# Gated linear attention from a hand-written list of steps: the front half of the list in another order

## The chip, the core and the metric

The kernel runs on one core of a Trainium2 chip. The metric is the device time of one execution in microseconds; the time before is the median of three runs. The engines are TensorE (PE, with its weight loads, PEld), VectorE (DVE), ScalarE (ACT), GpSimd (POOL) and SyncE (SP), which here only issues DMAs.

## The reference

Eight batches, eight heads, 576 tokens, 64 values a head; the model width is 512.

```python
q_s = np.exp(q - np.max(q, axis=-1, keepdims=True)); q_s = q_s / (np.sum(q_s, axis=-1, keepdims=True) + 1e-09)
k_s = np.exp(k - np.max(k, axis=2, keepdims=True));  k_s = k_s / (np.sum(k_s, axis=2, keepdims=True) + 1e-09)
kv = np.einsum('bhsd,bhse->bhde', k_s, v)
x  = np.einsum('bhsd,bhde->bhse', q_s, kv)          # then (batch, token, 512)
gate_pre = sum(conv_w[j] * x shifted by 4 - j tokens, j = 0 to 4)
gate = 1.0 / (1.0 + np.exp(-gate_pre))
out = (gate * (x @ w_val)) @ w_out
```

## The kernel before

The function lists its whole program in `ORDER`, 968 steps by name with a batch, a block of 128 channels and often a letter for the engine (a is ScalarE, v VectorE, p GpSimd). A loop calls the step's function for each, and no scheduler moves anything: every engine works through its own instructions in the order of the list, and waits, with all that stands behind, for data and for buffers. SyncE issues the loads and stores in the list's order too, and each DMA waits for the one eight places earlier.

One batch runs through these steps. `load_q`, `load_k`, `load_v` and others bring the data. The maximum of k over tokens is taken from strided loads (`load_km`, `k_peak`), goes to DRAM and back (`k_row`, `k_spread`) and is subtracted on GpSimd (`k_sub`), then ScalarE takes the exponential (`k_exp`, and `kt_exp` for the last 64 tokens). The first two batches take k by channels instead (`load_kc`, `k_top` on VectorE, `k_raise` on ScalarE) and turn it on TensorE (`k_turn`, `k_turned`). For q there are the maximum per head (`q_max`, VectorE), `q_sub` (GpSimd), `q_exp` (ScalarE) or `q_each` (both at once, ScalarE), the sums (`q_sum` or `q_total`, VectorE), and for batches 0 to 2 the scaling `q_mul`; `q_turn` transposes q on TensorE and `q_turned` copies it out of PSUM as `qT`. From batch 3 on `qT` comes from loads by channels (`load_qc`, `l_sub`, `c_exp`) with the logarithm of the sums (`q_log`, `l_turn`, `l_row`, `l_spread`).

`kv` is 80 matmuls; `kv_sums` and `kv_norm` on VectorE make `ks` and `kvd`. `attend` makes two blocks of x, 16 matmuls. Each block of x is split into a high part (`x_high`, a cast) and a low part (`x_low`, VectorE). The convolution of a block starts with `first` (one tap as a scaled copy), then three or four `tap`s on VectorE that add into the same tile `gate`; a `far` on ScalarE with a `near` on GpSimd can take a tap's place. For blocks 0 and 1 of batch 0 the convolution is made on TensorE (`conv_rows`, `conv_kv`, `conv`, tiles `dg`, `rows`, `cv`). `sigmoid` is a tanh on ScalarE (`conv_gate` for batch 0's two). `value` is a product of 24 matmuls with w_val, in three kinds (high part with low and high weights, low part with high weights); `gated` multiplies on VectorE (tile `g`), `g_high` and `g_low` split the result (`gh`, `gl`), `project` is the 24 matmuls with w_out, `copy` brings the result out of PSUM and `put` stores it.

The weights and tap weights arrive as 64-bit words. For each of eight slabs `part`, `field`, `scaled`, `signed` (two VectorE instructions) and `joined` build the float, and `w_high` and `w_low` split it; slabs 0 to 3 are w_val, 4 to 7 w_out. In the trace their tiles are `words`, `e` and `f`.

Buffers set further bounds: PSUM has four banks that rotate through all products in the list's order; `g` has two buffers, `gh` and `gl` four, the pair of x six, `gate` and `f` six, the big loads of q, k and v two each.

Of the kernel before, what the change touches and what calls it, by code (L numbers as in the profile page):

```python
# [37 lines left out]
    k_turn 0 1, load_km 2 2, load_words 2, field 1 p, q_each 0 0, conv_rows, signed 0, q_rec 0 2 5, scaled 1 a,
    q_mul 0 4 p, k_turned 0 1 v, k_turn 0 0, q_mul 0 2 p, load_km 2 1, k_tail_turn 0, q_sum 0 0 2, k_turned 0 0 a,
    q_eps 0 0 2 a, signed 1, load_kc 1 0, tail_turn 0, q_rec 0 0 2, part 1 a, load_kc 1 2, joined 1 v,  # L40
    tail_turned 0 v, load_q 1 0 5, k_tail_turned 0 a, kv 0, q_mul 0 1 a, k_peak 2 1, q_mul 0 0 p, q_mul 0 3 p,
    part 2 a, k_top 1 0, field 2 p, tail_high 0 a, k_top 1 2, kv_sums 0, q_turn 0 0, load_words 5, kv_norm 0 v,
# [1 line left out]
    joined 2 p, attend 0 0, field 5 p, w_high 1 a, q_max 1 0 2, attend 0 1, w_low 1 p, x_high 0 0 a, w_high 0 p,
    field 6 p, x_high 0 1 a, x_low 0 0, scaled 5 a, load_kc 1 1, w_low 0 p, load_words 7, first 0 3 a, load_km 2 3,
    joined 3 p, x_low 0 1, part 5 p, x_high 0 3 a, k_raise 1 2, field 7 p, q_max 1 2 4, tap 0 3 0, x_high 0 2 a,
    w_high 2 a, tap 0 3 2, conv, tap 0 3 1, q_each 1 3, first 0 2 a, tap 0 3 3, x_low 0 3, k_peak 2 2, q_sub 1 1 p,
    x_low 0 2, k_top 1 1, q_each 1 2, conv_gate 1, tail_high 1 p, k_peak 2 3, value 0 1, k_raise 1 0, signed 5,
    value 0 0, q_sub 1 0 p, load_kc 1 3, gated 0 1, q_exp 1 0 1, k_top 1 3, q_exp 1 1 2, load_vt 2, k_raise 1 1,
    load_words 4, joined 5 p, field 4 p, conv_gate 0, w_high 3 a, part 4 a, k_raise 1 3, q_sum 1 2 4, q_sum 1 0 2,  # L50
    q_eps 1 0 2 a, gated 0 0, scaled 4 p, q_rec 1 0 2, q_eps 1 2 4 a, signed 4, w_low 2 p, w_low 3 p, joined 4 p,
    k_turn 1 0, k_peak 2 0, tap 0 2 2, tap 0 2 1, load_km 3 0, q_mul 1 0 p, load_q 2 0 5, g_high 0 0 a, g_high 0 1 a,
# [704 lines left out]
```

## Time and profile before

| What | Time |
|---|---|
| median of three runs | 290.89 us (290.66 to 292.46) |
| the profiled execution | 291.31 us |
| its span in the profile | 289.5 us |
| busy: TensorE | 268.6 us (93% of the span) |
| busy: VectorE | 234.4 us (81%) |
| busy: GpSimd | 206.0 us (71%) |
| busy: ScalarE | 190.2 us (66%) |

The span begins with the first instruction of the profile and ends with the last; all times in rows are from the span's start. Time at which an engine is idle matters only where the engine that sets the end waits for it. The stretches that the rows use are these: 13.5 us is the first matmul, 34.9 us about the first value product, 143.4 us the kv products of batch 4, 286.5 us the last matmul.

### The profile page before, as it was taken

Reading aid. Unit: us, or ns where it says so; the run is one execution under the profiler, and the core shown is the slowest. Engines: PE = TensorE matmul, PEld = TensorE weight load, DVE = VectorE, ACT = ScalarE, POOL = GpSimd, SP = SyncE. Lnnn points to the kernel's source line nnn. Section 1 sums busy time; section 2 is a strip of 40 time slices with the busy share of each in tenths; the row PEclk is TensorE's granted clock in tenths of the full one; section 3 lists DMA queues with packets and bytes.
Section 4 is the critical chain, followed back from the end, with each engine's and each line's share of the span. In section 5 each row is a group of like instructions: output and inputs, shape, how many; then the busy total and the mean of one; then the engine's idle time right before and its main releaser. Section 6 shows DMA issues by size and latency. Waiting matters only on the chain.

```text
span 289.5 us, 6594 instructions
## 1 busy us (share of the span) xinstructions
PE 268.6 (93%) x2616; PEld 249.0 (86%) x2616; DVE 234.4 (81%) x334; ACT 190.2 (66%) x314; POOL 206.0 (71%) x187
## 2 busy tenths in 40 slices
PE   0188999899999999999999999999999999999995
PEld 0156599789998899898998898999989899989995
DVE  1999999999989979979788989799758974759620
ACT  2798989877598778563886774687936642655002
POOL 3657988789998989799299994879479284443300
PEclk9999999999999999999999999999999999999999
DMA  7999668988679799988869959954554800112022
GB/s 226 404 409 395 202 224 325 283 284 286 178 255 332 215 288 315 351 265 198 246 210 368 247 170 317 367 176 115 159 180 114 223 34 2 43 41 82 2 80 83
DMA packets 23462, 62.92 MB, mean 217 GB/s; under 512 B 3432, under 2 KB 3976, under 8 KB 20744
## 3 DMA queue, kind: packets, MB, share of 16 engines
q1 hardware_dynamic: 23432, 62.51, 66.0%
q8 instruction: 20, 0.33, 0.5%
q14 instruction: 10, 0.08, 0.1%
HBM read 52.96 MB, written 9.54 MB: 216 GB/s over the span
## 4 chain that ended last, share of the span: by engine, by line
PE 61%; DVE 18%; POOL 7%; ACT 5%; DMA 4%; issue 3%; SPq 0%; POOLq 0%; DVEq 0%; ACTq 0%
PE out_a L593 26%; PE val L593 26%; DVE gate L568 5%; PE kv L484 4%; PE x L543 4%; DMA out<-o 2%; DVE qs L412 2%; POOL k L318 2%; DVE e L263 2%; DVE kpk L303 1%; DMA words<-in_w_val 1%; DVE e L262 1%; DMA qc<-in_q_channels 1%; DVE ktop L339 1%; DVE g L652 1%
## 5 line engine op out<-in xcount | busy, mean ns | idle before, releaser
L593 PE MATMUL val<-x,w_val_hi 128*128 128x288 f32 x512 | 88.8, 295 | 0.0
L568 DVE SCALAR_TENSOR_TENSOR gate<-x,cw,gate 128x573 f32<-128x573 f32 (+3 forms) x98 | 78.4, 810 | 7.7 <-ACT gate L556 2.7
L593 PEld LDWEIGHTS val<-x,w_val_hi 128*128 128x128 f32 x512 | 75.2, 188 | 0.0
L593 PE MATMUL val<-x,w_val_lo 128*128 128x288 f32 x256 | 56.4, 301 | 0.6 <-DVE x L563 0.5
L593 PE MATMUL out_a<-gh,w_out_lo 128*128 128x288 f32 x248 | 54.6, 301 | 0.0
L593 PE MATMUL out_a<-gh,w_out_hi 128*128 128x288 f32 x248 | 53.2, 295 | 0.0
L660 POOL TENSOR_TENSOR gl<-g,gh 128x576 fp32r<-128x576 f32 x25 | 35.8, 1435 | 14.8 <-ACT gh L168 7.1
L593 PEld LDWEIGHTS out_a<-gh,w_out_lo 128*128 128x128 f32 x248 | 39.4, 188 | 5.3 <-ACT o L174 1.8
L593 PE MATMUL out_a<-gl,w_out_hi 128*128 128x288 f32 x248 | 43.2, 295 | 0.2 <-POOL gl L660 0.2
L593 PEld LDWEIGHTS val<-x,w_val_lo 128*128 128x128 f32 x256 | 40.7, 188 | 2.7 <-POOL f L176 1.0
L174 ACT ACTIVATE o<-out_a 128x576 f32<-128x576 f32 x27 | 17.6, 651 | 35.2 <-PE out_a L593 22.2
L593 PEld LDWEIGHTS out_a<-gh,w_out_hi 128*128 128x128 f32 x248 | 39.8, 188 | 0.0
L577 POOL TENSOR_TENSOR gate<-gate,far 128x573 f32<-128x573 f32 (+3 forms) x22 | 28.6, 1306 | 15.2 <-ACT far L573 7.6
L383 POOL TENSOR_TENSOR q<-q,qm 128x512 f32<-128x512 f32 x32 | 33.1, 1052 | 5.3 <-DVE qm L378 5.2
L593 PEld LDWEIGHTS out_a<-gl,w_out_hi 128*128 128x128 f32 x248 | 36.4, 188 | 0.4 <-POOL gl L660 0.4
L453 POOL TENSOR_TENSOR qc<-qc,lb 128x576 f32<-128x576 f32 (+1 forms) x17 | 24.7, 1465 | 13.6 <-DMA lb<-lrow 5.6
L652 DVE SCALAR_TENSOR_TENSOR g<-gate,val 128x576 f32<-128x576 f32 x32 | 23.9, 750 | 11.4 <-PE val L593 8.7
L318 POOL TENSOR_TENSOR k<-k,kmax 128x512 f32<-128x512 f32 x23 | 30.0, 1324 | 0.2
L563 DVE TENSOR_TENSOR x<-x,x 128x576 fp32r<-128x576 f32 x32 | 23.2, 750 | 1.8 <-ACT x L168 1.6
L573 ACT ACTIVATE far<-x,cw 128x574 f32<-128x574 f32 (+3 forms) x22 | 16.3, 739 | 12.4 <-PE x L543 4.8
L580 ACT ACTIVATE gate<-gate 128x576 f32<-128x576 f32 x30 | 19.8, 684 | 6.3 <-DVE gate L568 6.1
L556 ACT ACTIVATE gate<-x,cw 128x576 f32<-128x576 f32 x23 | 16.9, 742 | 6.7 <-PE x L543 5.0
(109 smaller groups left out, 443.2 us busy)
## 6 DMA issues: line engine op xcount, KB each, us to landing
out<-o SPq DMA_DIRECT2D x31, 288.0 KB, 2.8
v<-in_v SPq DMA_DIRECT2D x8, 1040.0 KB, 7.5
q<-in_q SPq DMA_DIRECT2D x7, 1024.0 KB, 7.6
km<-in_k_strided SPq DMA_DIRECT2D x24, 288.0 KB, 6.1
k<-in_k SPq DMA_DIRECT2D x6, 1024.0 KB, 6.3
qc<-in_q_channels SPq DMA_DIRECT2D x16, 288.0 KB, 7.7
lb<-lrow SPq DMA_DIRECT2D x8, 576.0 KB, 7.7
kc<-in_k_channels SPq DMA_DIRECT2D x8, 288.0 KB, 5.8
```

The lines of the kernel that those rows point to most:

```text
L174: nc.scalar.mul(out, in_, factor)
L318: engine(e).tensor_sub(kk[r, cs], kk[r, cs], mx[r, cs])
L383: engine(e).tensor_tensor(qq, qq, m, op=ALU.add if b < 2 else ALU.subtract)
L453: engine(e).tensor_sub(t, t, T["lb", b][:, p])
L556: nc.scalar.activation(a, x, AF.Copy, scale=w)
L563: nc.vector.tensor_sub(xl, T["x", b, p], T["xh", b, p].bitcast(F32))
L568: nc.vector.scalar_tensor_tensor(out=a, in0=x, scalar=w, in1=a, op0=ALU.mult, op1=ALU.add)
L577: nc.gpsimd.tensor_add(a, a, T["far", b, p, j])
L580: nc.scalar.activation(T["gate", b, p], T["gate", b, p], AF.Tanh, scale=0.5)
L593: nc.tensor.matmul(ps[:, cs], a[:, kb, ms], z[:, cs], start=(i == 0), stop=(i == len(parts) - 1))
L652: nc.vector.scalar_tensor_tensor(out=T["g", b, m], in0=T["gate", b, m], scalar=1.0, in1=T["val", b, m], op0=ALU.add, op1=ALU.mult)
L660: engine(e).tensor_sub(T["gl", b, m], T["g", b, m], T["gh", b, m].bitcast(F32))
```

## The change

Only `ORDER` differs, its lines 33 to 94, the first 551 steps. The remaining 417, from `k_spread 5, l_sub 4 3 p, kv 4` on, are the same. The functions are the same, and the steps of the front half are the same in number, except where a step changes its engine (54 of them, of the kinds `x_high`, `g_high`, `q_turned`, `k_turned`, `first`, `copy`, `q_mul`, `scaled`, `part`, `w_high`, `tail_high`) or a tap its way (`tap` or `far` with `near`; as many of each as before). Two lines of the 62, of before and after:

```diff
-    load_words 6, load_km 2 0, scaled 2 a, q_turn 0 1, conv_kv, q_turned 0 0 a, joined 0 p, signed 2, q_turned 0 1 a,
+    kv_sums 0, load_kc 1 2, field 2 p, scaled 2 p, kv_norm 0 v, q_turn 0 1, load_q 1 0 5, part 2 a, load_words 4,
```

In the instruction rows that follow, a name has the program's tile with its batch and block where it has them, and a number that tells buffers apart.

ScalarE, from the last two words passes of w_val to the casts of x in batch 0 (`e` and `f` are word slabs, `kc` is k by channels, `x_3` the product and `x_0_3` its split), before:

```order
L174 ACTIVATE f_299<-words_182 128x512
L168 COPY qT_305<-qTt_241 128x4x64
L174 ACTIVATE e_303<-e_303 128x512
L168 COPY qT_305<-qTps_0_311 128x2x512
L168 COPY qT_305<-qTps_1_329 128x2x512
L168 CAST w_val_hi<-f_236 128x4x128
L168 CAST x_0_0_371<-x_0_345 128x576
L168 CAST x_0_1_376<-x_1_346 128x576
L174 ACTIVATE e_355<-e_355 128x512
L556 ACTIVATE gate_3_385<-x_3_361,cw 128x576
L168 CAST x_0_3_393<-x_3_361 128x576
L343 ACTIVATE kc_2_238<-kc_2_238,ktop_301 128x576
```

After the change the same engine has these rows there:

```order
L174 ACTIVATE f_305<-words_144 128x512
L174 ACTIVATE f_328<-words_215 128x512
L168 COPY qT_252<-qTps_0_296 128x2x512
L168 COPY qT_252<-qTps_1_317 128x2x512
L168 CAST x_0_1_353<-x_1_342 128x576
L168 CAST x_0_0_355<-x_0_341 128x576
L556 ACTIVATE gate_3_370<-x_3_358,cw 128x576
L168 CAST x_0_3_377<-x_3_358 128x576
L168 CAST w_val_hi<-f_328 128x4x128
L168 CAST w_val_hi<-f_305 128x4x128
L556 ACTIVATE gate_2_388<-x_2_357,cw 128x576
```

The pass of `e` ahead of the two copies of `qT` is GpSimd's now, the other pass of `e` stands later in the list, and the cast of `w_val_hi` and the second of its kind stand behind the casts of x and the `first` of block 3.

VectorE, the same stage, before:

```order
L262 TENSOR_SCALAR e_303<-e_303 128x512
L263 SCALAR_TENSOR_TENSOR e_303<-words_182,e_303 128x512
L378 TENSOR_REDUCE qm_358<-q_243 128x16
L563 TENSOR_TENSOR x_0_0_371<-x_0_345,x_0_0_371 128x576
L563 TENSOR_TENSOR x_0_1_376<-x_1_346,x_0_1_376 128x576
L378 TENSOR_REDUCE qm_358<-q_243 128x16
L568 SCALAR_TENSOR_TENSOR gate_3_385<-x_3_361,cw,gate_3_385 128x572
L568 SCALAR_TENSOR_TENSOR gate_3_385<-x_3_361,cw,gate_3_385 128x574
L568 SCALAR_TENSOR_TENSOR gate_3_385<-x_3_361,cw,gate_3_385 128x573
L568 SCALAR_TENSOR_TENSOR gate_3_385<-x_3_361,cw,gate_3_385 128x575
L563 TENSOR_TENSOR x_0_3_393<-x_3_361,x_0_3_393 128x576
```

After the change the same engine has these rows there:

```order
L262 TENSOR_SCALAR e_312<-e_312 128x512
L263 SCALAR_TENSOR_TENSOR e_312<-words_215,e_312 128x512
L266 ISA f_305<-e_206,f_305 128x1024
L378 TENSOR_REDUCE qm_367<-q_326 128x16
L563 TENSOR_TENSOR x_0_1_353<-x_1_342,x_0_1_353 128x576
L563 TENSOR_TENSOR x_0_0_355<-x_0_341,x_0_0_355 128x576
L378 TENSOR_REDUCE qm_367<-q_326 128x16
L568 SCALAR_TENSOR_TENSOR gate_3_370<-x_3_358,cw,gate_3_370 128x573
L568 SCALAR_TENSOR_TENSOR gate_3_370<-x_3_358,cw,gate_3_370 128x574
L568 SCALAR_TENSOR_TENSOR gate_3_370<-x_3_358,cw,gate_3_370 128x575
L568 SCALAR_TENSOR_TENSOR gate_3_370<-x_3_358,cw,gate_3_370 128x572
L563 TENSOR_TENSOR x_0_3_377<-x_3_358,x_0_3_377 128x576
```

The join of a slab (`ISA`, tile `f`) stands between the word steps and the maximum of q; four taps of one block follow each other in both.

VectorE, around the sums of batch 1's kv (`ks`, `kvd`), before:

```order
L378 TENSOR_REDUCE qm_650<-q_580 128x40
L303 TENSOR_REDUCE kpk_658<-km_2_655 128x1
L652 SCALAR_TENSOR_TENSOR g_2_697<-gate_2_455,val_2_620 128x576
L170 COPY qT_473<-qTps_0_687 128x2x512
L493 TENSOR_SCALAR ks_755<-kv_711 128x4
L494 RECIPROCAL ks_755<-ks_755 128x4
L500 TENSOR_TENSOR kvd_762<-kv_711,ks_755 128x256
L652 SCALAR_TENSOR_TENSOR g_3_764<-gate_3_385,val_3_661 128x576
```

After the change the same engine has these rows there:

```order
L170 COPY k_577<-kps_1_631 128x4x256
L378 TENSOR_REDUCE qm_684<-q_627 128x40
L652 SCALAR_TENSOR_TENSOR g_2_689<-gate_2_388,val_2_641 128x576
L652 SCALAR_TENSOR_TENSOR g_3_709<-gate_3_370,val_3_597 128x576
L493 TENSOR_SCALAR ks_754<-kv_713 128x4
L494 RECIPROCAL ks_754<-ks_754 128x4
L500 TENSOR_TENSOR kvd_757<-kv_713,ks_754 128x256
L303 TENSOR_REDUCE kpk_771<-km_2_693 128x1
```

The copy of `qT` has left the place ahead of `ks`, and the gate product `g_3` has come ahead of it.

ScalarE, around the exponentials of k of batch 3 (L322) and of q of batch 4 (L387), before:

```order
L174 ACTIVATE o_1_1442<-out_1_a 128x576
L573 ACTIVATE far_2_3_1446<-x_2_1346,cw 128x575
L322 ACTIVATE k_1088<-k_1088 128x2048
L168 COPY qT_1462<-qTt_1205 128x4x64
L580 ACTIVATE gate_0_1255<-gate_0_1255 128x576
L174 ACTIVATE o_2_1499<-out_2_a 128x576
L387 ACTIVATE q_1299<-q_1299 128x2560
L456 ACTIVATE qT_1462<-qc_1_1361 128x512
```

After the change the same engine has these rows there:

```order
L174 ACTIVATE o_1_1490<-out_1_a 128x576
L580 ACTIVATE gate_1_1270<-gate_1_1270 128x576
L168 COPY qT_1501<-qTt_1124 128x4x64
L580 ACTIVATE gate_0_1268<-gate_0_1268 128x576
L387 ACTIVATE q_1334<-q_1334 128x2560
L322 ACTIVATE k_584<-k_584 128x2048
L456 ACTIVATE qT_1501<-qc_0_1389 128x512
L580 ACTIVATE gate_3_1367<-gate_3_1367 128x576
```

The exponential of k has moved from four places ahead of that of q to directly behind it. On TensorE the kv products of batch 3 stand behind three value products of batch 2 after the change, before it behind one.

## Rows read from the trace of the kernel before

**Rows 1.** by stretch: `start:end` in us and length, then busy us by engine, granted clock, DMA

```profile
13.50:34.90 21.40, 18.66 (x240) 13.01 (x240) 20.72 (x32) 20.20 (x50) 16.38 (x18) 1.00 0.90 345
34.90:143.40 108.50, 106.97 (x1016) 100.30 (x1016) 100.27 (x139) 81.58 (x138) 94.26 (x83) 1.00 0.85 270
143.40:286.50 143.10, 142.98 (x1361) 135.69 (x1360) 106.07 (x151) 81.72 (x115) 88.53 (x71) 1.00 0.48 153
```

**Rows 2.** TensorE's waits over the run: total us, times, longest us

```profile
PE kps L350 <- ACT kc L343: 13.5, 1, 13.5
...
PE cv L639 <- DVE x L563: 0.7, 1, 0.7
```

**Rows 3.** TensorE timeline: start us, duration us, line, operation, count, [idle before <-releaser]

```profile
34.94 0.51 PE L593 MATMUL val<-x,w_val_lo 128*128 128x288 f32 x2 [0.49 <-DVE x L563]
...
53.75 1.09 PE L509 MATMUL qTps<-ident,q 128*128 128x128 f32 x8
55.64 1.20 PE L543 MATMUL x<-qT,kvd 64*64 64x288 f32 x16 [0.79 <-DVE kvd L500]
...
108.35 0.69 PE L484 MATMUL kv<-v,k 128*64 128x65 f32 x16 [0.38 <-issue]
...
125.13 0.53 PE L593 MATMUL out_a<-gl,w_out_hi 128*128 128x288 f32 x2 [0.18 <-POOL gl L660]
```

**Rows 4.** ScalarE (ACT) and GpSimd (POOL) timeline around 23 to 30 us

```profile
24.15 0.64 ACT L174 ACTIVATE e<-e 128x512 f32<-128x512 f32 x1 [0.31 <-POOL e L253]
...
26.49 0.63 ACT L168 CAST w_val_hi<-f 128x512 fp32r<-128x512 f32 x1
...
28.94 0.63 ACT L174 ACTIVATE e<-e 128x512 f32<-128x512 f32 x1 [0.65 <-POOL e L253]
29.48 0.73 ACT L556 ACTIVATE gate<-x,cw 128x576 f32<-128x576 f32 x1
...
23.45 0.67 POOL L253 TENSOR_SCALAR e<-words 128x512 f32<-128x512 f32 x1
```

**Rows 5.** VectorE (DVE) timeline: conv stage, around 54 us, around 99 us

```profile
20.88 0.69 DVE L266 CUSTOM_DVE_ANT_0 f<-e,f 128x1024 uint16<-128x1024 uint16 x1
...
25.73 0.42 DVE L262 TENSOR_SCALAR e<-e 128x512 int32<-128x512 int32 x1
...
26.80 1.21 DVE L378 TENSOR_REDUCE qm<-q 128x16 f32<-128x1024 f32 x1
27.92 1.41 DVE L563 TENSOR_TENSOR x<-x,x 128x576 fp32r<-128x576 f32 x2
29.25 1.21 DVE L378 TENSOR_REDUCE qm<-q 128x16 f32<-128x1024 f32 x1
30.77 3.37 DVE L568 SCALAR_TENSOR_TENSOR gate<-x,cw,gate 128x572 f32<-128x572 f32 x4 [0.30 <-ACT x L168]
34.05 0.75 DVE L563 TENSOR_TENSOR x<-x,x 128x576 fp32r<-128x576 f32 x1
...
53.53 1.22 DVE L170 COPY qT<-qTps 128x1024 f32<-128x1024 f32 x1
54.66 0.15 DVE L493 TENSOR_SCALAR ks<-kv 128x4 f32<-128x4 f32 x1
...
99.26 0.81 DVE L568 SCALAR_TENSOR_TENSOR gate<-x,cw,gate 128x574 f32<-128x574 f32 x1
99.99 0.75 DVE L563 TENSOR_TENSOR x<-x,x 128x576 fp32r<-128x576 f32 x1
```

**Rows 6.** ScalarE, VectorE and SyncE queue (SPq) timeline, 86 to 110 us

```profile
103.49 1.91 ACT L322 ACTIVATE k<-k 128x2048 f32<-128x2048 f32 x1
...
109.73 2.34 ACT L387 ACTIVATE q<-q 128x2560 f32<-128x2560 f32 x1 [1.47 <-POOL q L383]
...
96.54 2.81 DVE L378 TENSOR_REDUCE qm<-q 128x40 f32<-128x2560 f32 x1
...
86.90 0.33 SPq L206 DMA_DIRECT2D q<-in_q  x1
```

More of the change, by code (lines that the diff above doesn't have):

```diff
@@ L38 @@
[L38 to L42, printed above, removed]
@@ L43 @@
-    load_words 6, load_km 2 0, scaled 2 a, q_turn 0 1, conv_kv, q_turned 0 0 a, joined 0 p, signed 2, q_turned 0 1 a,
[L44 to L52, printed above, removed]
@@ new lines @@
+    q_each 1 3, conv, w_low 1 p, q_sub 1 1 p, w_high 3 p, w_high 0 a, w_low 3 p, tap 0 3 2, x_high 0 2 a, tap 0 3 3,
+    load_km 2 0, part 5 a, w_low 0 p, load_kc 1 1, tap 0 3 0, load_kt 2, load_words 7, scaled 5 a, x_low 0 3,
+    k_top 1 1, k_top 1 2, conv_gate 1, x_low 0 2, q_exp 1 1 2, k_top 1 0, value 0 1, k_raise 1 1, scaled 4 a,
+    value 0 0, load_km 2 3, tap 0 2 0, signed 5, tap 0 2 2, gated 0 1, k_raise 1 0, field 6 p, load_kc 1 3,
+    q_each 1 2, q_sub 1 0 p, tail_high 1 a, part 4 a, joined 5 p, conv_gate 0, k_top 1 3, k_turn 1 0, q_sum 1 2 4,
@@ new lines @@
+    scaled 7 p, g_low 0 0 p, part 6 a, q_turn 1 0, gated 0 3, q_turned 1 0 a, w_low 5 p, kv 1, kv_sums 1,
+    kv_norm 1 v, g_high 0 2 a, q_turn 1 1, w_low 4 p, k_peak 3 2, g_low 0 2 p, scaled 6 a, attend 1 0, k_peak 4 3,
+    q_turned 1 1 a, g_high 0 3 a, first 1 0 a, g_low 0 3 p, signed 6, load_k 2, first 1 1 a, tap 1 0 3, tap 1 0 1,
+    load_q 3 0 5, tap 1 1 3, joined 6 p, project 0 1, x_high 1 0 a, w_high 6 a, tap 1 0 0, tap 1 1 0, copy 0 1 a a,
+    k_spread 2, x_high 1 1 a, tap 1 0 2, q_sub 2 4 p, project 0 0, x_low 1 0, w_low 6 p, load_km 6 2, tap 1 1 1,
@@ new lines @@
+    put 0 1, attend 1 1, q_sub 2 3 p, copy 0 0 a a, part 7 a, tap 1 1 2, x_high 1 3 a, load_vt 2, signed 7,
+    x_low 1 1, load_vt 4, q_sub 2 2 p, joined 7 p, first 1 2 a, q_sub 2 0 p, x_low 1 3, x_high 1 2 a, q_sub 2 1 p,
+    load_km 4 1, project 0 2, far 1 2 2, x_low 1 2, load_km 4 2, w_high 7 a, load_v 2, w_low 7 p, tap 1 2 1,
+    q_max 3 0 4, value 1 0, k_sub 2 1 p, q_sub 3 1 p, load_km 3 3, tap 1 2 3, k_sub 2 4 p, sigmoid 1 0, first 1 3 a,
+    copy 0 2 a a, project 0 3, q_exp 2 0 5, gated 1 0, q_sum 2 0 5, k_peak 3 0, kt_exp 2, q_sub 3 0 p, q_eps 2 0 5 a,
@@ new lines @@
+    copy 1 0 a a, k_peak 5 0, first 2 3 a, x_high 2 2 a, l_row 3, tap 2 0 1, tap 2 0 2, k_sub 3 3 p, x_low 2 0,
+    q_max 4 0 5, k_sub 3 0 p, first 2 2 a, put 1 3, put 1 0, far 2 0 0, load_v 4, k_sub 3 4 p, load_qc 3 0,
+    project 1 2, k_peak 5 1, project 1 1, q_sub 4 3 p, x_low 2 2, q_sub 4 2 p, x_high 2 3 a, tap 2 2 1, l_spread 3,
+    tap 2 3 1, x_low 2 3, copy 1 2 a a, value 2 1, tap 2 2 2, q_sub 4 1 p, near 2 0 0, tap 2 3 3, k_peak 5 3,
+    kt_exp 3, q_sub 4 0 p, k_peak 6 1, q_sub 4 4 p, copy 1 1 a a, sigmoid 2 1, gated 2 1, tap 2 3 0, g_high 2 1 p,
```

88 lines of the change are left out of this document (41 added, 47 removed).

## The prediction

> **What bounds the kernel now.** I read the busy time of each engine by stretch first [rows 1]. Up to 13.5 us TensorE has nothing to do (it waits for ScalarE's last raised block of k, [rows 2]). From 13.5 to 34.9 us it works 18.66 of 21.4 us, from 34.9 to 143.4 us 106.97 of 108.5 us, and from 143.4 to 286.5 us, where the list of steps is the same before and after, 142.98 of 143.1 us. The granted clock is 1.00 throughout. So after 13.5 us TensorE is the bound, and the reader should see how little is left there: 2.74 us of idle time in the first stretch that it works in and 1.53 us in the second, 4.27 us together. A new order of the same work can shorten the run only out of these 4.27 us, out of the 13.5 us of start, and out of short gaps that lie under the modelled ends of matmuls. The same rows say what could lengthen it: from 34.9 to 143.4 us VectorE is busy 100.27 and GpSimd 94.26 of 108.5 us, so neither has much room to run ahead.
>
> Next come the waits of TensorE [rows 2] and their places on its timeline [rows 3]. In the middle of the conv products 0.7 us go for the low half of x. The first value product starts at 34.94 after 0.49 us, the x products of batch 1 at 55.64 after 0.79 us, the kv products of batch 3 at 108.35 after 0.38 us, and one pair of an out product of batch 2 at 125.13 after 0.18 us.
>
> **The change, part by part.** The arithmetic, the matmuls and the taps are the same in number; 54 front steps change engine and nearly all change place. The pieces that reach TensorE are these.
>
> *Start to 13.5 us: nothing.* The same loads, maxima, subtractions and exponentials stand ahead of the first transposes; `rows` now runs before them instead of between, in TensorE's idle time. I take 0; the loads decide here, and with more of them early the first transposes may be some tenths of a microsecond earlier or later.
>
> *The conv stage, 24 to 35 us: −0.65 us.* The value product at 34.94 waits for the low halves of x on VectorE. Followed back from there [rows 4, 5]: `x_low` starts at 34.05, behind four dependent taps from 30.77 (3.28 us for four, 0.82 each), which waited 0.30 us for ScalarE's cast of x, the step behind 29.48. ScalarE was late because it stood 0.65 us in front of a word scaling (28.94) that needed GpSimd, and before that 0.31 us in front of another (24.15); the weight cast at 26.49 cost 0.63 us more. After, the first of these scalings is GpSimd's, the second stands some steps later, and the weight cast is behind x. ScalarE then comes to the `first` of block 3 at about 27.9 instead of 29.48, and the cast is done by 28.6. VectorE becomes the limit: GpSimd's word pass starts at 23.45 and takes 0.67 us [rows 4], its scaling as long again, so VectorE has its two word steps from 24.8 on (1.07 us from 25.73 to 26.80 [rows 5]), then the joining step that was moved here (0.69, from 20.88), the q maximum (1.12, from 26.80 to 27.92), two `x_low` (1.33, from 27.92 to 29.25) and the other maximum (1.12 again). That is 24.8 + 5.33 = 30.1 instead of 30.77 for the first tap, 0.65 us. The taps are as dependent as before, so all behind them moves by as much, and the value product starts at about 34.3. The copy of qT stays ScalarE's, so the x products of batch 0 start when they did, to 0.2 us.
>
> *The x products of batch 1: −0.79 us.* The copy of qT on VectorE from 53.53 to 54.66 stood ahead of the reciprocal sums at 54.66 [rows 5], though kv was done at 53.75, when the transposes of q began [rows 3]. After, that copy is ScalarE's, and the gate product that followed the sums stands ahead of them. The sums can start when kv ends, 0.9 us earlier, more than the 0.79 us that TensorE waited. The price: the second gate product needs a buffer that GpSimd's low half of block 0 frees, with about 2 us to spare by the durations of the steps ahead of it.
>
> *Small gaps, −0.56 to −1.16 us.* The 0.38 us ahead of kv 3 and the 0.18 us in out 2 0 belong to places that are rebuilt. Beside these, the starts of the second value product of batch 1 and of the x products of batch 3 stand some 0.25 and 0.35 us later than the matmuls ahead of them would need; the modelled ends cover that, so no view calls it a wait, and these 0.6 us are my estimate. I take all 1.16 as gone, since the neighbours changed at each place.
>
> The gross sum is 0.65 + 0.79 + 1.16 = 2.6 us.
>
> *New waits, +0.5 to +1.0 us.* I walked the new order by hand with the durations of the trace; the delays below are that walk's estimates. Places where what TensorE wants is not ready, or just ready: the second half of x of batch 2 waits for a bank whose copy is now half VectorE's (0.25 us); out 1 1 waits for a bank that a scaled copy on ScalarE reads (0.3); x of batch 3 waits for its predecessor (0.3); the low half of block 2 for out 2 0 comes late, because the logarithm's difference and four transposes stand ahead of its gate product on VectorE (0.5); and x 3 1 waits for a tap (0.45). Those sum to 1.8 us. My walk left out about 0.1 us at each change of the kind of product, so TensorE really comes to these places 1 us or more later, which eats about half. I take 0.8.
>
> *Dependent neighbours on VectorE: nothing on the path.* An independent tap at 99.26 lets the next instruction start 0.73 us later; four dependent ones take 0.82 each [rows 5]. The order of after has 71 pairs in which an instruction reads what the one ahead wrote, that of before 78: 7 × 0.09 = 0.6 us of VectorE, spread over 143 us in which VectorE is not what TensorE waits for most of the time. As a bound from both sides: 0, and 0.6 us if each pair were on the path; I take 0.
>
> [...]
>
> *From kv 4 on: nothing.* The tail's steps are the same, and TensorE is gapless there [rows 1]; what is gained before 143.4 us arrives at the end, unless a step on another engine is then late for TensorE. It has 142.98 of 143.1 us busy, so the others kept up in that order.
>
> Net: 2.6 − 0.8 = 1.8 us. The profiled run took 291.31 us (its span is 289.5), the median is 290.89, so it stands 0.42 us above. 291.31 − 1.8 = 289.5, and on the scale of the median **289.1 us**.
>
> **The rivals.**
>
> *All of the gain stays.* The new waits vanish in the gaps that my walk omitted: 290.89 − 2.6 = 288.3, and if all 4.27 us of idle time went, 286.6, the very best. For it speaks that ScalarE has spare time (81.58 of 108.5 us); against it that VectorE and GpSimd have little.
>
> *The gain is given back.* TensorE comes 1.4 us earlier to 56 us, but VectorE and GpSimd have the same work and are busy 92 and 87% of the stretch up to 143.4 us [rows 1]; where they set the pace, TensorE waits for them. The places are the five above, with the whole 1.8 us or up to the gross 2.6: 290.1 to 290.9.
>
> *The other side: kv 3 waits for q.* Before, the exponential of k of batch 3 ran on ScalarE at 103.49, ahead of that of q of batch 4 at 109.73 [rows 6]. After it stands directly behind q's, which takes 2.34 us and waits for five GpSimd subtractions, these for the maximum of q of batch 4 (VectorE, 96.54 to 99.26, with no wait ahead of it) and that for its load (issued at 86.90, so 9.6 us before). By my walk k's exponential ends at 112.0 and kv 3 wants it at 112.25: 0.2 us to spare. The load of q now stands directly behind a whole v in SyncE's queue. If the maximum starts after about 98.9 us, each microsecond is lost on TensorE whole. Late by 3 us gives 289.1 + 3 = 292.1, and for over 1% slower it has to be 5 us: 294.1. Against it: the load has some 10 us from its issue to the maximum in the new order too.
>
> *The title's reason alone.* If the dependent neighbours were what counts, VectorE's 0.6 us would be the whole gain: 290.89 − 0.6 = 290.3.
>
> **How the numbers follow.** A measurement of this kernel tells about 1% (2.9 us) from no change, so faster is under 288.0, slower over 293.8. Chances: my forecast, 288.3 to 289.9, 0.40; all of the gain, 286.6 to 288.3, 0.18; given back 0.16, or the title's reason alone 0.08, 289.9 to 291.2; kv 3, 291.2 and more, 0.18, of which half goes over 293.8. Faster takes most of the second case, 0.15; slower 0.09; the rest, 0.76, is within 1%. The range leaves out the best tenth and the worst tenth: 287.2 to 292.4.
>
> **What would show it.** The first value product at about 34.3 us, with a wait of VectorE's x about as before. No wait of the x products of batch 1 for `kvd`, and x at about 54.2 us. kv 3 without a wait for ScalarE's k. kv 4 starting near 141.6 us, and the stretch from there to the end 146.1 us long, as before. The forecast is wrong if the first transposes move by more than half a microsecond, if out 2 0 or x 3 1 wait for a microsecond, or if kv 3 waits for k.

## The result and the profile after

The changed kernel takes 288.49 us in the median (288.14 to 289.04, five runs), the kernel before 290.89. The ratio is 0.990, with an interval of 0.987 to 0.993. A later set of runs of the same kernel (a0) gave 0.991 (0.988 to 0.995). The forecast was 289.1 us.

The profiled execution took 289.04 us, 2.27 less than that of before (291.31). TensorE by stretch, in the columns of [rows 1]:

```profile
13.50:34.30 20.80, 18.65 (x245) 12.87 (x246) 19.59 (x31) 20.38 (x51) 16.28 (x18) 1.00 1.01 401
34.30:54.40 20.10, 19.80 (x213) 18.70 (x216) 19.72 (x29) 19.23 (x49) 16.50 (x17) 1.00 0.62 187
54.40:141.40 87.00, 86.46 (x812) 81.03 (x806) 80.22 (x111) 66.03 (x100) 78.04 (x67) 1.00 0.86 274
```

From 13.5 us to the kv products of batch 4 TensorE is idle for 2.15 + 0.30 + 0.54 = 2.99 us, where it was 4.27 [rows 1]: 1.28 us less. That stretch is 127.9 us long instead of 129.9. The other 0.7 us show in no view as a wait: the busy sum fell from 125.63 to 124.91 us with the same work in it. I take them for gaps that the ends of matmul rows cover, since a row of two value matmuls is given 0.43 us (33.98) where the next row starts 0.27 us behind it (34.25). They lie late in the front: from x of batch 1 to kv of batch 4 the busy time fell from 87.17 to 86.47 us, the idle time only from 0.63 to 0.54.

TensorE's waits over the run, in the columns of [rows 2]:

```profile
PE rows L617 <- POOL dg L609: 13.3, 1, 13.3
PE x L543 <- ACT qT L168: 0.7, 1, 0.7
PE cv L639 <- DVE x L563: 0.6, 1, 0.6
PE kv L484 <- ACT k L168: 0.5, 1, 0.5
PE out_a L593 <- POOL gl L660: 0.3, 1, 0.3
PE out_a L593 <- ACT far L573: 0.2, 1, 0.2
PE kps L350 <- DVE g L652: 0.2, 1, 0.2
PE qTps L509 <- POOL q L471: 0.2, 1, 0.2
```

Four waits of before are gone: that of the first value product, that of the x products of batch 1 for `kvd`, that of kv 3 (0.49, 0.79 and 0.38 us in [rows 3]), and 0.52 us that the tail part of kv of batch 0 waited for ScalarE's `ktz`. Their places and the landmarks on TensorE's timeline after:

```profile
25.07 2.17 PE L543 MATMUL x<-qT,kvd 64*64 64x288 f32 x32 [0.65 <-ACT qT L168]
...
33.64 0.50 PE L593 MATMUL val<-x,w_val_lo 128*128 128x288 f32 x2
...
50.50 0.69 PE L484 MATMUL kv<-v,k 128*64 128x65 f32 x16
...
54.14 1.20 PE L543 MATMUL x<-qT,kvd 64*64 64x288 f32 x16
...
112.68 0.69 PE L484 MATMUL kv<-v,k 128*64 128x65 f32 x16
...
123.22 0.54 PE L593 MATMUL out_a<-gl,w_out_hi 128*128 128x288 f32 x2 [0.32 <-POOL gl L660]
...
141.15 0.69 PE L484 MATMUL kv<-v,k 128*64 128x65 f32 x16
```

Where the time came from is read from landmarks that both traces have:

| TensorE | before | after | moved by |
|---|---|---|---|
| first x product of batch 0 | 25.73 | 25.07 | −0.66 |
| first value product | 34.94 | 33.64 | −1.30 |
| kv of batch 1 | 51.27 | 50.50 | −0.77 |
| x of batch 1 | 55.64 | 54.14 | −1.50 |
| kv of batch 4 | 143.44 | 141.15 | −2.29 |
| end of the execution | 291.31 | 289.04 | −2.27 |

The lines of before that [rows 3, 4] lack: ScalarE's copy of qT of batch 0, for which x of batch 0 waits, and the kv products of batches 1 and 4:

```profile
24.69 1.91 ACT L168 COPY qT<-qTps 128x1024 f32<-128x1024 f32 x2
...
51.27 0.69 PE L484 MATMUL kv<-v,k 128*64 128x65 f32 x16
...
143.44 0.69 PE L484 MATMUL kv<-v,k 128*64 128x65 f32 x16
```

So the front of the program gained 1.30 us, lost 0.53 of them again up to kv of batch 1, got 0.73 more at x of batch 1, and 0.79 between there and kv 4. From kv 4 to the end both take the same, 147.9 us. The profiled run of a0, the same kernel, agrees up to the first value product (20.28 us behind the first matmul, here 20.31, before 21.44), but it loses nothing up to kv of batch 1: that stretch takes 16.10 us there, 16.86 here and 16.33 before.

Behind these steps stand the following rows: GpSimd's and VectorE's timelines in the conv stage, and ScalarE's there and around 110 us:

```profile
20.67 2.05 POOL L471 TENSOR_TENSOR q<-q,qs 128x512 f32<-128x512 f32 x2 [1.37 <-DVE qs L406]
22.69 0.67 POOL L253 TENSOR_SCALAR e<-words 128x512 f32<-128x512 f32 x1
23.44 0.62 POOL L176 TENSOR_SCALAR e<-e 128x512 f32<-128x512 f32 x1
...
23.30 0.82 DVE L624 TENSOR_TENSOR dg<-rows,kvd 128x640 f32<-128x640 f32 x1
24.10 0.43 DVE L262 TENSOR_SCALAR e<-e 128x512 int32<-128x512 int32 x1
...
29.47 3.35 DVE L568 SCALAR_TENSOR_TENSOR gate<-x,cw,gate 128x573 f32<-128x573 f32 x4
32.74 0.75 DVE L563 TENSOR_TENSOR x<-x,x 128x576 fp32r<-128x576 f32 x1
34.54 1.41 DVE L339 TENSOR_REDUCE ktop<-kc 128x1 f32<-128x576 f32 x2 [1.05 <-DMA kc<-in_k_channels]
...
24.03 1.89 ACT L168 COPY qT<-qTps 128x1024 f32<-128x1024 f32 x2
...
110.48 1.90 ACT L322 ACTIVATE k<-k 128x2048 f32<-128x2048 f32 x1
```

The word pass of GpSimd starts at 22.69 (23.45 before, [rows 4]), VectorE's word steps at 24.10 (25.73, [rows 5]), the four taps at 29.47 (30.77), ScalarE's copy of qT at 24.03 (24.69). Behind `x_low` (32.74) VectorE stands idle for 1.05 us, because k by channels has not landed.

### The profile page after: what moved, and what is told of

It reads as the page before. It is cut to its first block, busy times and chain, and to the rows that moved or that the text cites. A ratio compares the mean times of both kernels' runs of the same rounds, so it can differ in the third digit from the quotient of the medians.

```text
span 287.3 us, 6606 instructions
## 1 busy us (share of the span) xinstructions
PE 267.8 (93%) x2616; PEld 248.2 (86%) x2616; DVE 231.5 (81%) x332; ACT 191.6 (67%) x323; POOL 206.2 (72%) x187
## 4 chain that ended last, share of the span: by engine, by line
PE 65%; DVE 13%; DMA 8%; POOL 6%; ACT 4%; issue 3%; SPq 0%; DVEq 0%; POOLq 0%; ACTq 0%
PE out_a L593 31%; PE val L593 25%; PE x L543 4%; DMA kc<-in_k_channels 4%; PE kv L484 3%; DMA kt<-in_k_tail 3%; POOL gl L660 2%; DVE gate L568 2%; DVE ktop L339 1%; ACT q L469 1%; DMA words<-in_w_val 1%; POOL q L471 1%; DVE g L652 1%; DVE e L263 1%; DVE qs L393 1%
## 5 line engine op out<-in xcount | busy, mean ns | idle before, releaser
L568 DVE SCALAR_TENSOR_TENSOR gate<-x,cw,gate 128x575 f32<-128x575 f32 (+3 forms) x98 | 78.3, 808 | 4.8 <-ACT gate L556 1.9
L577 POOL TENSOR_TENSOR gate<-gate,far 128x572 f32<-128x572 f32 (+3 forms) x22 | 29.0, 1320 | 16.4 <-DVE gate L568 8.1
L174 ACT ACTIVATE o<-out_a 128x576 f32<-128x576 f32 x26 | 16.9, 651 | 29.3 <-PE out_a L593 22.6
L573 ACT ACTIVATE far<-x,cw 128x572 f32<-128x572 f32 (+3 forms) x22 | 16.2, 739 | 12.5 <-PE x L543 4.7
L168 ACT CAST x<-x 128x576 fp32r<-128x576 f32 x27 | 17.0, 640 | 7.3 <-PE x L543 4.2
```

Of the source, the lines that this page charges most:

```text
L168: nc.scalar.copy(out=out, in_=in_)
L174: nc.scalar.mul(out, in_, factor)
L568: nc.vector.scalar_tensor_tensor(out=a, in0=x, scalar=w, in1=a, op0=ALU.mult, op1=ALU.add)
L577: nc.gpsimd.tensor_add(a, a, T["far", b, p, j])
```

## The experiments

All ratios are to the kernel before, on the same chip as the kernel in question; the intervals are those of 95%. Of each edit the parts of lines that differ are shown; `...` stands for what is left out.

| Kernel | made from | ratio |
|---|---|---|
| a0, the changed kernel again | after | 0.991 (0.988 to 0.995) |
| e1, the copy of qT alone | before | 1.006 (1.002 to 1.010) |
| e7, the copy, word steps later | before | 1.008 (1.005 to 1.011) |
| e9, the copy, maxima first | before | 1.002 (0.999 to 1.005) |
| g1, the order of after up to the first value product | before | 1.008 (1.005 to 1.011) |
| b3, b4, the conv stage alone (two versions) | before | 1.013 (1.009 to 1.016), 1.003 (1.001 to 1.005) |
| e4, more dependent neighbours | after | 0.998 (0.996 to 1.001) |
| e2, e5, v of batch 1 loaded later | after | 0.990 (0.987 to 0.993), 0.990 (0.987 to 0.994) |

Two more (b1, e8) were run once each, 292.66 and 291.33 us, and are used for their timelines.

**Is the copy of qT what the x products of batch 1 waited for?** The kernel before, with that copy on ScalarE:

```diff
-    q_turned 1 0 v,
+    q_turned 1 0 a,
```

> The kernel before with one letter changed: the copy of qT of batch 1's first half goes from VectorE to ScalarE, at its old place in the list. Theory (step of the x products of batch 1): VectorE reaches the sums of kv 1.13 us earlier, TensorE's wait of 0.79 us for kvd is gone, and the x products start at about 54.9 instead of 55.64 us; the gain arrives at the end, 0.7 to 0.8 us (ratio to before 0.9974). Rival (given back): VectorE or GpSimd set the pace of the next stages, kv 2 starts at 81.2 as before and the time changes by less than 0.2 us.

x of batch 1 starts at 54.63 without a wait, 1.0 us earlier (0.79 counted from the first matmul), as expected; and yet the whole is slower, which neither theory had. VectorE and GpSimd right behind it:

```profile
55.29 1.22 DVE L262 TENSOR_SCALAR e<-e 128x512 int32<-128x512 int32 x1
56.54 1.90 DVE L263 SCALAR_TENSOR_TENSOR e<-words,e 128x512 int32<-128x512 int32 x1
...
54.81 1.42 POOL L660 TENSOR_TENSOR gl<-g,gh 128x576 fp32r<-128x576 f32 x1 [0.76 <-ACT gh L168]
56.47 1.43 POOL L660 TENSOR_TENSOR gl<-g,gh 128x576 fp32r<-128x576 f32 x1 [0.24 <-ACT gh L168]
```

The two word steps of a slab take 1.22 and 1.90 us. In the kernel before the same two take 0.42 and 0.71, since a `gl` has ended or has not begun when they start:

```profile
56.07 0.42 DVE L262 TENSOR_SCALAR e<-e 128x512 int32<-128x512 int32 x1
56.52 0.71 DVE L263 SCALAR_TENSOR_TENSOR e<-words,e 128x512 int32<-128x512 int32 x1
...
54.40 1.42 POOL L660 TENSOR_TENSOR gl<-g,gh 128x576 fp32r<-128x576 f32 x1 [0.15 <-ACT gh L168]
56.94 1.58 POOL L660 TENSOR_TENSOR gl<-g,gh 128x576 fp32r<-128x576 f32 x1 [1.12 <-ACT gh L168]
```

In e1 each starts while GpSimd works on a `gl` and ends 0.3 and 0.5 us behind its end. 2.0 us of VectorE go there, in a stretch in which it has no room. The taps, the split of x and the second x products follow, and kv of batch 2 starts 1.24 us later than before. That the wait goes was right; that it was worth 0.8 us was not.

**Can the collision be moved away?** Two kernels, both with the same copy on ScalarE. In e7 the word steps stand behind three taps, in e9 just behind two maxima of k, which is their place in the kernel after.

```diff
-    attend 1 0, project 0 1, signed 6, first 1 1 a, first 1 0 a, joined 6 p, k_peak 3 0, load_k 2, k_peak 3 3,
+    attend 1 0, project 0 1, first 1 1 a, first 1 0 a, k_peak 3 0, load_k 2, k_peak 3 3,
...
-    q_turned 1 1 a, tap 1 0 1, tap 1 0 3, part 7 a, k_spread 2, x_high 1 0 a, tap 1 1 3, w_high 6 a,
+    q_turned 1 1 a, tap 1 0 1, tap 1 0 3, part 7 a, k_spread 2, x_high 1 0 a, tap 1 1 3, signed 6, joined 6 p, w_high 6 a,
```

> The kernel before with the copy of qT of batch 1's first half on ScalarE, and with the two word steps of slab 6 on VectorE (and the join on GpSimd that needs them) moved behind three taps. Without that move the two steps took 1.22 and 1.90 us instead of 0.42 and 0.69, beside GpSimd's low halves of the out products, and the kernel became 0.6% slower. Theory (contention between VectorE and GpSimd): moved to a time at which GpSimd has nothing, the steps take 0.42 and 0.69 us again, the x products of batch 1's second half start at 62.5 us or earlier with no wait, and the gain of the copy arrives: 0.6 to 1.0 us shorter than before (ratio 0.9965 to 0.998). Rival (ScalarE has no room for the copy): the second half of x still waits for ScalarE's copy of an out product, and the time stays over that of before (ratio 1.003 or more).

The word steps are back at 0.42 and 0.69 us, but the taps now wait for the scaled copy of ScalarE, which stands behind the copy of qT, and the next pair of word steps collides instead. VectorE and TensorE:

```profile
58.41 2.39 DVE L568 SCALAR_TENSOR_TENSOR gate<-x,cw,gate 128x573 f32<-128x573 f32 x3 [1.25 <-ACT gate L556]
...
65.56 1.64 DVE L263 SCALAR_TENSOR_TENSOR e<-words,e 128x512 int32<-128x512 int32 x1
...
66.70 0.54 PE L593 MATMUL out_a<-gh,w_out_lo 128*128 128x288 f32 x2 [1.02 <-POOL w_out_lo L291]
```

The rival's ratio came true, its account only in part: the second x products (64.25) wait 1.14 us for VectorE's split, not for ScalarE's copy of an out product. The edit has a price of its own too, as GpSimd's join moved along with the word steps: ScalarE waits 2.52 us for it with the cast of w_out, which the 1.02 us above follow. e9, in the same terms:

```diff
-    attend 1 0, project 0 1, signed 6, first 1 1 a, first 1 0 a, joined 6 p, k_peak 3 0, load_k 2, k_peak 3 3,
+    attend 1 0, project 0 1, first 1 1 a, first 1 0 a, k_peak 3 0, load_k 2, k_peak 3 3, signed 6, joined 6 p,
```

> The kernel before with the copy of qT of batch 1 on ScalarE, and on VectorE the two maxima of k (kpk) ahead of the two word steps (L262, L263) instead of behind them, the order that the kernel after has there. With the copy alone the word steps ran beside GpSimd's low half (gl) and took 1.22 and 1.90 us. Theory A, their collision is what the copy's move costs: the first word step now starts at about 56.4 us, at the same time as or ahead of the second gl, the two take 0.42 and 0.69 us, the taps start at about 57.5 us (58.45 before the change), x of batch 1 starts about 1 us earlier than before without a wait for kvd, and the whole takes 290.0 to 290.7 us where the kernel before takes 291.3: a ratio of 0.995 to 0.998. Theory B, it isn't enough: ScalarE, with the 1 us copy ahead of the cast for the low half, has no room, or the collision turns up at the next pair; the taps or the split of x wait for it, and the ratio is 1.002 or more.

VectorE and GpSimd:

```profile
56.33 0.42 DVE L262 TENSOR_SCALAR e<-e 128x512 int32<-128x512 int32 x1
56.78 1.80 DVE L263 SCALAR_TENSOR_TENSOR e<-words,e 128x512 int32<-128x512 int32 x1
...
56.41 1.62 POOL L660 TENSOR_TENSOR gl<-g,gh 128x576 fp32r<-128x576 f32 x1 [0.25 <-ACT gh L168]
```

The first word step was ahead of `gl`, the second came 0.37 us behind its start and paid 1.1 us. In the kernel after the second word step starts at 55.71, 0.21 us ahead of `gl` at 55.92; there it takes 0.69 us and GpSimd pays, 1.78 us instead of 1.42. In these rows the one that begins second is the longer for it. The ratio, 1.002, stands at the edge of theory B's figures and outside theory A's, and a difference to before isn't shown: of e1's loss, 1.8 us between the medians, 0.7 are left, and of its 2.0 us of collision 1.1.

**The conv stage: what let VectorE start earlier?** GpSimd's two scalings of q took 2.05 us after and 2.49 before, when a join of VectorE (20.88, [rows 5]) started beside them. b1 moves that join alone:

```diff
-    load_kc 1 2, joined 1 v, tail_turned 0 v,
+    load_kc 1 2, tail_turned 0 v,
...
-    k_top 1 2, kv_sums 0,
+    k_top 1 2, joined 1 v, kv_sums 0,
```

> The kernel before with one VectorE step moved: the join of slab 1 (20.88 us in before, beside two of GpSimd's q scalings) comes after two maxima of k, when GpSimd's scalings are done. Theory: the join slowed the scalings (2.49 us for two, elsewhere 2.05); they take 2.05 us again and GpSimd's pass of the words of slab 2 starts 0.4 us earlier, 9.5 us after the first matmul instead of 9.95. TensorE's first value product does not move by more than 0.2 us, since VectorE's sums stand where they did. Rival: the two scalings keep 2.49 us, so their length comes from something else, such as the loads.

GpSimd and VectorE:

```profile
20.96 2.05 POOL L471 TENSOR_TENSOR q<-q,qs 128x512 f32<-128x512 f32 x2 [1.37 <-DVE qs L406]
...
23.62 1.27 POOL L266 TENSOR_TENSOR f<-e,f 128x512 int32<-128x512 int32 x1
...
23.61 1.82 DVE L266 CUSTOM_DVE_ANT_0 f<-e,f 128x1024 uint16<-128x1024 uint16 x1
```

The scalings fall to 2.05 us, as expected. The join, now beside another GpSimd step, takes 1.82 us instead of 0.69, `ks` and x of batch 0 come later, and the first value product starts at 36.23, where no more than 0.2 us of change was expected. The join and that step start within 0.01 us of each other. The collision was shown, and moved (from GpSimd's 0.44 us to VectorE's 1.13), not removed.

b4 makes the whole conv stage of the kernel before like that of after (join behind the word steps, one scaling on GpSimd, the weight casts and the other scaling behind x, two `k_top` behind `x_low`); two of its places:

```diff
-    conv_kv, q_turned 0 0 a, joined 0 p, signed 2, q_turned 0 1 a,
+    conv_kv, q_turned 0 0 a, signed 2, joined 1 v, q_turned 0 1 a,
...
-    scaled 2 a,
+    scaled 2 p,
```

> The kernel before with the conv stage of after alone, mended: in the last such kernel GpSimd waited 4.05 us for a buffer ahead of the low half of weight slab 1, and TensorE 4.07 us for that; here the low halves of slabs 1 and 0 stand ahead of the steps that need the buffer, and the join of slab 0 stands behind that of slab 2, away from VectorE's word steps. Both theories expect the first value product 0.9 to 1.4 us earlier (20.0 to 20.5 us after the first matmul; in before 21.44). Theory A (gains add): the x products of batch 1 start 0.7 us earlier or more (41.4 us after the first matmul or less, in before 42.14) and the run is 0.7 us or more shorter (ratio below 0.9975). Theory B (VectorE and ScalarE pace the stretch behind it): the x products start 41.7 us after the first matmul or later, and the time is within 0.5 us of before.

> The kernel before with the conv stage of after alone: the scaling of slab 2 on GpSimd, the join of slab 1 behind the word steps of slab 2, the weight cast and the scaling of slab 5 behind the casts of x, two maxima of k behind the taps; all behind it as in before. Both theories expect the first value product 1.0 to 1.4 us earlier (20.0 to 20.4 us after the first matmul, before 21.44). Theory A (gains add): VectorE's wait chain up to the x products of batch 1 moves along, and the run is 0.8 to 1.4 us shorter (ratio 0.995 to 0.9975). Theory B (the front is paced by VectorE and ScalarE, and an early TensorE only waits later): the x products of batch 1 still start 41.6 to 42.2 us after the first matmul (before 42.14), and the time is within 0.4 us of before or longer.

In b3 the rotation of the buffers gave a part of a slab a buffer that a maximum of k still read; GpSimd waited 4.05 us for it, the first value product came at 38.91, and it says nothing on the question. In b4 the value product starts at 34.50, 0.44 us ahead of [rows 3] and 0.31 counted from the first matmul, where both theories wanted 0.9 to 1.4. VectorE, ahead of its word steps, stands idle for kv of batch 0, whose tail still waits 0.54 us for ScalarE's `ktz`, and TensorE waits at two places behind the value product:

```profile
23.41 0.16 DVE L493 TENSOR_SCALAR ks<-kv 128x4 f32<-128x4 f32 x1 [1.07 <-PE kv L484]
...
43.75 0.66 PE L350 MATMUL kps<-ident,kc 128*128 128x128 f32 x4 [1.10 <-ACT kc L343]
...
56.64 1.20 PE L543 MATMUL x<-qT,kvd 64*64 64x288 f32 x16 [0.87 <-DVE kvd L500]
```

The first of TensorE's is k by channels, whose maxima were moved back to make room; the second is still the copy of qT, since this kernel leaves it on VectorE. From the first matmul x of batch 1 is 43.27 us away, before it was 42.14. That is theory B's side; its time (within 0.5 us) was not met, with 0.8 us between the medians. Since little more than 0.3 us were gained in front, the kernel says less than planned on what an earlier front is worth.

g1 takes all of the order of after up to the first value product, with the rest of before behind it (what the first part has left out comes in the old order):

```diff
-    k_top 1 1, q_each 1 2, conv_gate 1, tail_high 1 p, k_peak 2 3, value 0 1, k_raise 1 0,
...
+    k_top 1 1, k_top 1 2, conv_gate 1, x_low 0 2, q_exp 1 1 2, k_top 1 0, value 0 1, field 6 p, load_km 2 3,
+    k_raise 1 2, field 7 p, q_each 1 2, tail_high 1 p, k_peak 2 3, k_raise 1 0,
```

> The order of after up to the first value product, and from there the order of before with the steps left out that have been done. Theory: the front alone brings the first value product to 33.6 us (1.3 us earlier), and most of it arrives: kv 4 starts 0.9 to 1.3 us earlier than in before, at 142.1 to 142.5, and the run is shorter by as much (ratio 0.9955 to 0.997). Rival (given back): before's order behind it is paced by VectorE up to 55.6 us, the x products of batch 1 start at 55.4 or later, and the time falls by less than 0.3 us.

The value product starts at 34.56, 0.65 us earlier than before counted from the first matmul (1.13 in the kernel after), but `kps` then waits 1.91 and 0.59 us for ScalarE's k by channels, and x of batch 1 starts at 58.75. TensorE, and the granted clock in 40 equal slices of the span:

```profile
43.54 1.24 PE L350 MATMUL kps<-ident,kc 128*128 128x128 f32 x8 [1.91 <-ACT kc L343]
...
PEclk9999997999999999999999999999999999999999
```

Part of the loss is the clock's. In one slice, 43.8 to 51.1 us, behind the first wait and across the second, the granted clock is 0.7 to 0.8 of full speed, in all others 0.9 or more; its mean over the execution is 0.993. The rows of two value matmuls at 46.76, 47.24 and 47.72 are given 0.68 us instead of 0.43 and start 0.48 us apart instead of 0.27; from 48.68 on they are as elsewhere. One of the seven executions kept a mean of 1.00 and still took 292.83 us. With before's order behind it the front alone gains nothing.

**Dependent neighbours.** From the kernel after, the taps of three batches regrouped so that seven more pairs of neighbours depend on each other, 35 instead of 28 of taps; one of three places:

```diff
-    tap 1 0 3, tap 1 0 1, ... tap 1 1 3, ... tap 1 0 0, tap 1 1 0, ... tap 1 0 2,
+    tap 1 0 3, tap 1 0 1, ... tap 1 0 0, ... tap 1 0 2, tap 1 1 3, ... tap 1 1 0,
```

> The kernel after with taps of the same block put next to each other again at three places (batches 1, 2 and 3), by exchanging taps among their own places in the list: 35 pairs of neighbouring taps in which the second reads what the first wrote, instead of 28, about as many as before has. Theory: VectorE is busy 0.5 to 0.7 us more and TensorE sees next to none of it; the time is within 0.2 us of after (ratio to before 0.990). Rival (the reason in the title): the gain of the change lies in these pairs, and the time goes up by 0.6 us or more (ratio 0.992 or above).

The kernel took 290.73 us (289.54 to 292.40), some 2 us more than the kernel after. My figure of 0.2 us was wrong and the rival's, 0.992 or above, came true; but it isn't the dependence that the trace shows. VectorE and ScalarE in e4:

```profile
59.55 1.54 DVE L568 SCALAR_TENSOR_TENSOR gate<-x,cw,gate 128x574 f32<-128x574 f32 x2 [0.71 <-ACT x L168]
61.80 0.81 DVE L568 SCALAR_TENSOR_TENSOR gate<-x,cw,gate 128x572 f32<-128x572 f32 x1 [0.71 <-ACT x L168]
...
58.88 0.64 ACT L168 CAST x<-x 128x576 fp32r<-128x576 f32 x1 [1.95 <-DVE gate L568]
```

The cast reads only x, and still waits for taps that read the same x: three taps end at 58.85, the cast runs from 58.88 to 59.52, and the next taps start at 59.55, in the order of the list. With the taps of a block in one row, the cast waits 1.95 us (1.10 in a0) and the taps then wait for the cast twice, 1.42 us together, with no tap of the other block between to fill the time. ScalarE in a0, where the taps alternate:

```profile
57.67 0.64 ACT L168 CAST x<-x 128x576 fp32r<-128x576 f32 x1 [1.10 <-DVE gate L568]
```

Against a0 `x_low` starts 1.64 us later, counted from x of batch 1; 1.42 of them are these two waits, which leaves about 0.2 us for the dependence. From x of batch 1 to kv 4 the kernel takes 88.26 us, a0 87.13: 1.13 us of the 1.52 between the two profiled runs; the rest stands ahead of the regrouped taps. So 0.09 us a pair, as in [rows 5], is not contradicted, but the run does not isolate it.

**The load of k by channels.** The 1.05 us of VectorE at 34.54 waits for a load of 288 KB that was issued at 22.86, 3.7 us behind the whole v of batch 1 (1040 KB, 19.12). In e2, and again in e5 beside a0, v stands behind it:

```diff
-    first 0 3 a, load_v 1, x_low 0 1,
+    first 0 3 a, x_low 0 1,
...
-    load_kc 1 1, tap 0 3 0,
+    load_kc 1 1, load_v 1, tap 0 3 0,
```

> The kernel after with the load of v of batch 1 (1040 KB) moved behind the load of k by channels 1 1 on SyncE. Theory: in after that load of k lands late (11.66 us after its issue, VectorE idle 1.05 us at 34.54), and this is why TensorE's lead shrinks from 1.30 us at the first value product to 0.63 us at the second transposes of q of batch 1; with v behind it VectorE does not wait, the x products of batch 1 start at 53.5 to 53.8 instead of 54.14, and the run is 0.3 to 0.6 us shorter than after (ratio to before 0.978 to 0.989, some 0.988). Rival: the lead is lost to the length of the chain on VectorE and ScalarE from 36 to 53 us and not to the load; the x products start at 54.1 and the time is that of after (ratio 0.990).

> The changed kernel itself, for comparison on the same chip with the other runs of this group. Expected: ratio to before 0.988 to 0.992, as it was.

> The kernel after with the load of v of batch 1 behind the load of k by channels 1 1, once more, on the same chip as the changed kernel. Theory: the x products of batch 1 start 0.9 us earlier than in after and all of it arrives, so the run is 0.7 to 1.1 us shorter than after (0.3%). Rival: no difference, within 0.3 us.

The wait is gone; VectorE in e2:

```profile
33.43 1.40 DVE L339 TENSOR_REDUCE ktop<-kc 128x1 f32<-128x576 f32 x2
```

From the first value product to kv 1 the profiled runs take the longer, the longer VectorE waits for this load:

| run | VectorE's wait | the stretch |
|---|---|---|
| after | 1.05 us | 16.86 us |
| e8 | 0.54 | 16.36 |
| e4 | 0.52 | 16.34 |
| a0 | 0.30 | 16.10 |
| e2, e5 (v behind) | none | 16.04, 16.03 |

With v ahead VectorE waited each time, with v behind it didn't; but how late the load lands differs between executions of one program (a wait of 1.05 us in after, 0.30 in a0), and against a0 the exchange brings nothing at x of batch 1 (40.19 us behind the first matmul in e5, 40.01 in a0). e5's theory is wrong there. The two kernels are shorter behind that point: x of batch 1 to kv 4 takes 86.38 and 86.32 us, in after and a0 87.01 and 87.13. GpSimd waits there 0.95 and 0.65 us for a load, in after and a0 2.61 and 2.70, and TensorE's wait for `gl` is gone. Whether that comes of the edit is open. e5 and a0 on one chip took 288.31 (287.70 to 290.43) and 288.93 us (288.49 to 289.42). It is the fastest order measured, but the ranges overlap, and that it beats the kernel after isn't shown.

**Rival three, kv 3 behind q.** From the kernel after, the maximum of q of batch 4 put later on VectorE:

```diff
-    x_low 2 0, q_max 4 0 5, k_sub 3 0 p,
+    x_low 2 0, k_sub 3 0 p,
...
-    tap 2 3 1,
+    tap 2 3 1, q_max 4 0 5, q_sub 4 3 p, q_sub 4 2 p,
```

> The kernel after with the maximum of q of batch 4 on VectorE moved behind four other VectorE instructions (two splits or maxima and two taps), so that it starts some 2.8 us later. Theory (the prediction's other side): in after the exponential of k of batch 3 ends at 112.38 and kv 3 starts at 112.68, so 0.3 us are to spare; the exponential of k ends at 115.0 to 115.4, kv 3 waits 2.2 to 2.7 us for it, and the run is longer than after by 2.0 to 2.7 us. Rival: the wait is caught up, since TensorE's later products find their data ready, and the run is longer by less than 1 us.

ScalarE and TensorE:

```profile
113.70 1.89 ACT L322 ACTIVATE k<-k 128x2048 f32<-128x2048 f32 x1
...
115.69 0.69 PE L484 MATMUL kv<-v,k 128*64 128x65 f32 x16 [2.48 <-issue]
```

Counted from x of batch 1, the maximum starts 2.95 us later than in a0. There the exponential of k ended 0.31 us ahead of kv 3; 2.95 − 0.31 = 2.64, and kv 3 waits 2.48 us. The delay arrives at kv 3 nearly whole. At kv 4 1.88 us of it are left, somewhat less than expected. The execution took 291.33 us, 2.4 more than a0's median; 0.7 us of that stand ahead of x of batch 1, where the edit changes nothing.

## Why the prediction came out right

**The size.** 289.1 was forecast, 288.5 measured; against the profiled execution −1.8 was forecast and −2.27 came. At x of batch 1 the sum was nearly exact (−1.44 forecast, −1.50 measured), but by two errors that cancel, and in this execution only. The number 54 was wrong: comparing the two lists gives 35 front steps on another engine; no term rests on it.

**Start: 0.** The first matmul, now `rows`, is at 13.33 instead of 13.50. Right to 0.2 us.

**Conv stage: −0.65 forecast, −1.30 measured.** The chain was right: VectorE is the limit, 24.10 + 5.33 = 29.43 by the prediction's own sum of steps, and the first tap starts at 29.47. The failed term is where the chain starts. I took VectorE's word steps from GpSimd's word pass at 23.45, as it stood before, and so had 24.8. Both engines were ready earlier. The join that I moved on VectorE had been slowing GpSimd: without it the two scalings of q are 0.44 us shorter and begin 0.31 us earlier, the pass starts at 22.69, and its scaling is done at 24.06. VectorE's own `dg` is done at 24.12: two maxima of k (1.40 us) stand behind the taps now, and kv of batch 0 is done 0.99 us earlier, of which 0.52 are the wait for ScalarE's `ktz`. This is read from the timelines. No run isolates it; b4, which has GpSimd's part and the maxima but not the earlier `ktz`, got its first tap only 0.30 us earlier from the first matmul, the kernel after 1.13.

x of batch 0, which I held to 0.2 us, starts 0.66 us earlier. It waits for ScalarE's copy of qT before and after (0.57 and 0.65 us), and that copy starts 0.66 us earlier, because the word scaling ahead of it, which waited for GpSimd at 24.15 [rows 4], has left ScalarE. I had that scaling's move in my chain and didn't follow it to the copy. The wait of the first value product, which I expected to stay, is gone: the conv products start at 27.82 instead of 28.73 and, at 5.73 us in both, end at 33.55, when the low half is ready too.

**Between the first value product and kv 1: nothing forecast, 0.53 us lost.** I followed what was ahead of the value product and gave the earlier start to everything behind. VectorE there needs k by channels, and its load is now behind a whole v. The stretch goes with VectorE's wait for that load in all six runs; a0, which waits 0.30 us, is 0.23 us faster there than before. So the loss is real in the profiled run, and no fixed cost of the order.

**x of batch 1: −0.79 forecast, and the wait is gone.** x starts at 54.14, against 54.2 forecast. But the reason as I priced it, a copy moved from a full engine to one with time to spare, is not a gain by itself: alone it makes the kernel 0.6% slower (e1). I named a buffer as its price and didn't look at what VectorE, set free 0.9 us earlier, would run beside. e7 and e9 show other prices, ScalarE's and the same collision in another place. In the kernel after the maxima of k, the order of the gate products, one scaling on GpSimd and a copy of k on VectorE are moved along. Which of them it takes was not separated.

**Small gaps and new waits: −1.16 + 0.8 = −0.36 forecast, −0.79 measured.** This is the term that made the forecast too high. kv 3's 0.38 us is gone, as I took it. Out 2 0 still waits for `gl`, 0.32 us at 123.22 instead of 0.18, and out 1 1 waits 0.21 for `far` at 99.69; both are among the five places that my walk named. x 3 1 and the x products of batches 2 and 3 don't wait. So the new waits were 0.53 us and not 0.8, and the gaps that no view shows, which I put at 0.6 us, gave 0.70 by the fall of the busy time. Ahead of out 2 0 GpSimd had waited 2.61 us for a load (up to 111.73), which my walk didn't have. Two waits that I didn't name, `qTps` at 22.77 and `kps` at 40.59, are 0.18 and 0.20 us; they lie ahead of x of batch 1.

**Dependent neighbours: 0.** VectorE's busy time fell from 234.4 to 231.5 us, more than the 0.6 of the dependent pairs. The rival that puts the whole gain down to them would have given 290.3; the time came out 1.8 us lower, and the landmarks place it elsewhere. The four taps of after, dependent, take 0.82 us each (29.47 to 32.74), as before. What stands behind the 0.82 against 0.73 us of [rows 5] no run here isolates. e4 shows that the order of taps can cost more than a microsecond in another way, by ScalarE's casts and VectorE's taps of one x waiting for each other (1.95 us of the cast, twice 0.71 of the taps), which I didn't price.

**The rivals.** kv 3 did not wait, with 0.30 us to spare (k ends at 112.38) where I had 0.2; e8 bears out the price of 1:1 at kv 3, but by kv 4 1.88 of 2.64 us are left. "Given back" did not come true for the whole kernel, but b4, g1 and e1, which take parts of it, all end later than before. "All of the gain" (288.3) lay nearer the result than my forecast.

**From kv 4 on: nothing.** 147.87 us before, 147.89 after, to the end of the execution.
